# GpSimd as a third elementwise engine, another charge for its overlap with VectorE, and k/q turned by two f32 matmuls

## The chip, the cores and the metric

The kernel runs on one core of a Trainium2 chip. A core has TensorE (matmuls, whose weights are loaded by instructions of their own), VectorE, ScalarE, GpSimd, and SyncE, which here issues every DMA. The metric is the time of one execution on the device in microseconds. The profile calls the engines PE (and PEld for the loads of weights), DVE, ACT, POOL and SP.

## The reference

Attention with a soft cap feeds a two-layer block with a leaky activation. There are 4 batches, 12 heads, 448 positions, a head size of 64, a model width of 768 and an inner width of 2048; all inputs are f32.

```python
scores = scale * np.matmul(q, k.transpose(0, 1, 3, 2))
scores = cap * np.tanh(scores / cap)
scores = scores - np.max(scores, axis=-1, keepdims=True)
attn = np.exp(scores)
attn = attn / (np.sum(attn, axis=-1, keepdims=True) + 1e-09)
x = matmul(attn, v), heads laid side by side: 1792 x 768
h = x @ w_in
g = np.maximum(h, 0.0) + alpha * np.minimum(h, 0.0)
out = g @ w_out
```

## The kernel before

**Precision.** Most products are done in f16 with each operand split in two: hi is the f16 value of the scaled operand, lo the f16 value of what hi misses. A product is then three matmuls, hi with hi, hi with lo and lo with hi. So q, k, v, the probabilities, w_in, w_out, the attention output and the activation g all pass through a split. There are two ways to split. The direct one scales and rounds to hi (`scaled`), then makes lo with one VectorE operation that scales, subtracts and rounds (`split_lo`, L389). The indirect one scales in place in f32 (`scaled`), copies to hi (`copy`), and subtracts (`minus`, L386), which GpSimd may do as well as VectorE. `QA`, `VA`, `AI` and `AO` say which share of the tensors of q/k, of v, of w_in and of w_out goes the direct way; `share(i, x)` spreads it evenly. In the kernel before, q/k, w_in, w_out and the probabilities are all direct, v half.

**Batch 0** is computed in f32 (`attention32`), because its units come before much else can run. A unit is a pair of heads in one of two parts of the sequence (192 and 256 rows). `turn` (L449 to L455) brings k and q from rows to columns: for each chunk of 112 rows one transpose on TensorE for the first head (L454) and one f32 matmul with the identity for the second (L455), which puts it on the other half of the output partitions. The scores are f32 matmuls (L666). The probabilities are turned by f32 matmuls with a diagonal matrix that also scales them (`turn_32`, L561), and multiplied with v in f32 (`PV_32`, L611). `PD_A` and `PD_B` say from which pair on, in each part, a unit takes the f16 way instead: with 5 in the second part it is the last of its six pairs.

**Batches 1 to 3** (`attention`, 18 units) split q and k into the tile nat, turn it by one DMA transpose into qkTs, form the scores from it in f16 (L724), take tanh, maximum, exp and sum (`steps`, L508, L513, L515, L520, L525), split each block of 128 rows of probabilities into pw (`turn_split`), and turn pw by DMA transposes into ptall, from which `PV_split` (L597) makes the output with the split v.

**The block after it.** `mm1` (L741) makes h for 128 inner columns at a time, 18 matmuls each, then scales, applies the activation (L751), and splits into gall. `mm2` (L782) makes the output rows from gall and w_out. The weights come in with `w_in_chunks` and `w_out_all`: the words are turned into f32 (L837, L841, L847), scaled by norms (L861), and split in `split_w`.

**The order of the work** is written out when the program is built. Every piece of work is handed to `Plan.op` with a priority, a table of engines that may do it and its cost there in ns, and the regions that it reads and writes. `Plan.order` plays this through as an event simulation: a free engine takes the ready piece of lowest priority number, with a penalty (`PEN`, `PEN2`) added where VectorE is one of several choices; `emit` then issues the instructions in that order on the engines chosen. All DMAs are on SyncE's queue in the planned order. While TensorE has nothing ready, up to a planned time `FILL_END`, the planner gives it filler matmuls (L991) that nobody reads. A VectorE piece has `port=True` unless it reads PSUM or reduces; in the kernel before the plan lets such a piece and a GpSimd piece follow one another but never overlap. On the chip only semaphores for data hold the engines back.

Of the kernel before, what the change touches and what calls it, by code (L numbers as in the profile page):

```python
# [26 lines left out]
PD_B = 5  # L27
MQ = 3
AQ = 3
PEN = 593.1  # L30
PEN2 = 357.34
B0_P = -21.6
LD_P = -4.13
LO_P = -146.94
MM_P = 766.13
X_P = 30.7
ST_P = -12.3
ST1_P = 9.3
PV_P = 53.98
QK_P = -5.54  # L40
V_P = 27.5
WI_P = 31.8
WI_S = 4.16
A_S = 12.4
MM1_P = 6.26
WO_P = 75.25
WO_S = 5.62
WT_P = -127.9
WT_S = -15.47
B1_P = 46.83  # L50
B_S = 32.07
EVAC_P = 201.2
# [7 lines left out]
AI = 1  # L60
AO = 1
PW = 3
QA = 1.0
VA = 0.5
FILL_END = 365429.37
# [10 lines left out]
class Plan:  # L76
# [42 lines left out]
    def order(self):  # L119
# [8 lines left out]
        port = {"dve": 0.0, "pool": 0.0}  # L128
# [23 lines left out]
        def put(o):  # L152
            for e in o.times:
                heapq.heappush(ready[e], (o.prio + ((PEN if "act" in o.times else PEN2) if len(o.times) > 1 and e == "dve" else 0.0), o.idx, o))

# [8 lines left out]
        while todo:  # L164
            while events and events[0][0] <= now:
                _, _, kind, x = heapq.heappop(events)
                if kind == 0:
                    for y in x.next:
                        y.deps -= 1
                        if not y.deps:  # L170
                            put(y)
                elif kind == 1:
                    banks.append(x.slot)
                    used[x.kind] -= 1
            for e in free:
# [3 lines left out]
                while ready[e]:  # L179
# [14 lines left out]
                    if e == "sp":  # L194
                        issue, wait, t = t
                        dma = max(now + wait, dma) + t
                        end = dma + 1000.0 - LAT
                        lanes = lanes[1:] + [dma + 1000.0]
                        free[e] = max(now + issue, lanes[0])
                    else:  # L200
                        free[e] = end = run_pe(t, o.rows) if e == "pe" else now + t
                        if e == "pool":
                            free[e] = end = port[e] = max(now, port["dve"]) + t
                        elif e == "dve" and o.port:
                            port[e] = end
# [3 lines left out]
                    seq += 1  # L209
                    heapq.heappush(events, (end + LAT, seq, 0, o))  # L210
                    for h in o.handles:
                        h.ops.remove(o)
                        if not h.ops:
                            seq += 1
                            heapq.heappush(events, (end + LAT, seq, 1, h))
# [22 lines left out]
def kernel(  # L238
# [39 lines left out]
    alph = ct([P, NF], F32, "alph")  # L278
    n_wi = ct([P, NF], F32, "n_wi")
# [4 lines left out]
    sg = ct([P, NF], F32, "sg")  # L284
    cs_g = ct([P, NF], F32, "cs_g")
    ca_g = ct([P, NF], F32, "ca_g")
# [104 lines left out]
    def either(n, psum=False):  # L391

        return {"act": 220 + 0.85 * n, "dve": 170 + (1.05 if psum else 0.5) * n}
# [143 lines left out]
    def turn_split(u, pr, n, c, t, tr, f, fr):  # L537
# [5 lines left out]
        op(pr, {"act": 640, "dve": 470}, lambda e: scaled(e, hi, t, f), r=[*tr, fr], w=[wt[0]])  # L543
        op(pr, {"dve": 680}, lambda e: split_lo(lo, t, f, hi), r=[*tr, fr, wt[0]], w=[wt[1]])
# [6 lines left out]
    def turn_32(u, pr, n, c, t, tr, f, fr):  # L551
# [4 lines left out]
        op(pr, either(P), lambda e: scaled(e, d, ident, f), r=[identr, fr], w=[dr])  # L556
# [12 lines left out]
    def split(prio, raw, rr_, sv, st, hi, hr, lo, lr, direct):  # L569

        if direct:
            op(prio, two, lambda e: scaled(e, hi, raw, sv), r=[rr_, st], w=[hr])
            op(prio, {"dve": 740}, lambda e: split_lo(lo, raw, sv, hi), r=[rr_, st, hr], w=[lr])
            return
        op(prio, two, lambda e: scaled(e, raw, raw, sv), r=[st], w=[rr_])
        op(prio, two, lambda e: copy(e, hi, raw), r=[rr_], w=[hr])
        op(prio, {"pool": 1370, "dve": 650}, lambda e: minus(e, lo, raw, hi), r=[rr_, hr], w=[lr])
# [7 lines left out]

    two = {"act": 710, "dve": 485}

    def PV_split(u, prio, n, vs, vt):
# [11 lines left out]
        op(prio, {"pe": 12 * (n / 2.4 + 3)}, PV, r=vt + [("pt", u.po[x], u.po[x] + 4 * n) for x in range(2)], w=[h])  # L600
# [17 lines left out]
    def xout(u, prio, h, w, o, sc, sr=()):  # L618
# [7 lines left out]
        op(prio, either(w, True), part(lambda e, pv: scaled(e, hi, pv, sc)), r=[h, *sr], w=[xr(u.b, u.pair, 0, o, w)], port=False)  # L626
        op(prio, {"dve": 247 + 0.82 * w}, part(lambda e, pv: split_lo(lo, pv, sc, hi)),
# [4 lines left out]
    def attention32(part, pair):  # L632
# [6 lines left out]
        if part == 0:  # L639
            h = plan.handle("a")  # L640
            rk, rkr = raw32[4, pair]
            op(prio, {"pe": 1720}, lambda e, h=h: turn(h, rk, 0, NCH), r=[rkr, identr], w=[h], rows=0.7)
# [9 lines left out]
        op(prio, {"pe": 430 * nch}, lambda e, h=h: turn(h, rq, c0, nch), r=[rqr, identr], w=[h, qr], rows=0.7)  # L652
# [26 lines left out]
    def attention(b, pair):  # L679
# [47 lines left out]
        steps(u, prio, S, S_, lambda c: 430 if c == 3 else 380, [qt], [sc, amt], True)  # L727
# [5 lines left out]
    def mm1(b, j, o, n, prio):  # L733
# [16 lines left out]
        op(pr, either(n, True), lambda e: scaled(e, t, ps_p[h.slot][:, :n], cs_g[:, j:j + 1]), r=[h] + sgt, w=[tt], port=False)  # L750
# [3 lines left out]
        for src, to, m in pieces:  # L754
# [3 lines left out]
            op(pr + 10, either(m), lambda e, hi=hi, a=a: copy(e, hi, t[:, a]), r=[tt], w=[gh])  # L758
            op(pr + 10, {"pool": 420 + 1.6 * m, "dve": 160 + 0.97 * m}, lambda e, hi=hi, lo=lo, a=a: minus(e, lo, t[:, a], hi),
# [15 lines left out]
    def mm2(b, t, hf, prio):  # L775
# [19 lines left out]
        op(EVAC_P + prio * 1e-4, either(NH, True), lambda e: scaled(e, osb[:, cols], ps_p[h.slot][:, :NH], osc),  # L795
# [80 lines left out]
    def split_w(prio, dst, dr, flat, fr, s, sr, direct):  # L876
        space, a, z = dr
        high, low = (space, a, (a + z) // 2), (space, (a + z) // 2, z)
        if direct:
            op(prio, {"act": 930, "dve": 545}, lambda e: scaled(e, dst[:, :DM], flat, s), r=[fr, sr], w=[high])  # L880
            op(prio, {"dve": 960}, lambda e: split_lo(dst[:, DM:], flat, s, dst[:, :DM]), r=[fr, sr, high], w=[low])
# [49 lines left out]


# [106 lines left out]
```

## Time and profile before

| | |
|---|---|
| median of 3 runs | 751.47 us (751.47 to 752.59) |
| span of the profiled execution | 749.1 us |
| TensorE busy | 718.3 us, 96% |
| VectorE busy | 514.4 us, 69% |
| ScalarE busy | 450.0 us, 60% |
| GpSimd busy | 156.6 us, 21% |

The profiled execution's own time is given by its span, from the first to the last instruction; the runs are timed around the whole launch. Busy is the time in which an engine has an instruction in work. A matmul in the pipeline counts until its modelled end, so TensorE can show as busy with short gaps inside. Fillers count as busy.

### The profile page before, as it was taken

To read this page: it belongs to the slowest core of one execution; us is meant where nothing else is said; L and a number is where in the kernel's file an instruction comes from. 1 tells how busy PE (TensorE), PEld (TensorE's weight loads), DVE (VectorE), ACT (ScalarE), POOL (GpSimd) and SP (SyncE) were. 2 spreads that over 40 slices of the span, in tenths; PEclk is the share of its full clock that TensorE was granted. 3 is DMA by queue.
4 is the path that set the end of the run, shared out by engine and by line. 5 is a ranking of instruction groups with operands and counts; after the bars stand their busy time and mean duration, and the time that the engine had idled before them with its cause. 6 is when DMAs were issued, how large, how long until landed. Compare 5 with 4: busy or idle time off the path is not lost.

```text
span 749.1 us, 13417 instructions
## 1 busy us (share of the span) xinstructions
PE 718.3 (96%) x5043; PEld 446.5 (60%) x5043; DVE 514.4 (69%) x1021; ACT 450.0 (60%) x893; POOL 156.6 (21%) x286
## 2 busy tenths in 40 slices
PE   9999999967987999999999999999999999999997
PEld 5776576656865875566545556555455555555664
DVE  2889889898897888867787787777877642452000
ACT  3768778874796786577775666688576632231010
POOL 1012112141442241102434211213343100000000
PEclk9999999998999999999999999999999999999999
DMA  9956525576988647998648699998736960000001
GB/s 213 279 177 210 163 92 179 95 186 165 188 154 181 99 100 152 192 182 159 114 87 160 123 192 213 179 176 137 145 72 118 157 120 1 21 1 1 22 22 42
DMA packets 227936, 98.66 MB, mean 132 GB/s; under 512 B 191456, under 2 KB 224160, under 8 KB 227872
## 3 DMA queue, kind: packets, MB, share of 16 engines
q1 hardware_dynamic: 227872, 97.82, 62.1%
q8 instruction: 39, 0.64, 0.4%
q14 instruction: 25, 0.20, 0.1%
HBM read 45.82 MB, written 5.51 MB: 69 GB/s over the span
## 4 chain that ended last, share of the span: by engine, by line
PE 83%; DMA 8%; DVE 5%; ACT 2%; issue 1%; POOL 0%; SPq 0%; ACTq 0%; POOLq 0%
PE p L782 27%; PE p L741 25%; PE s L724 6%; PE p L597 5%; DMA ptall<-pw 4%; PE p L561 4%; PE s L666 4%; PE p L991 4%; DMA qkTs<-nat 3%; PE p L611 2%; PE p L455 2%; PE p L454 1%; PE p L861 1%; PE p L365 1%; DVE wi L389 1%
## 5 line engine op out<-in xcount | busy, mean ns | idle before, releaser
L741 PE MATMUL p<-xring,wi 128*128 128x448 f16 (+2 forms) x1440 | 229.1, 319 | 6.5 <-DVE gr L751 5.8
L782 PE MATMUL p<-wp,gall 128*128 128x384 f16 x1344 | 225.3, 326 | 0.0
L741 PEld LDWEIGHTS <-wi 128*128 128x128 f16 x1440 | 137.6, 99 | 93.7 <-issue 11.7
L782 PEld LDWEIGHTS <-gall 128*128 128x128 f16 x1344 | 129.9, 98 | 90.6 <-issue 5.7
L389 DVE SCALAR_TENSOR_TENSOR pw<-tall,rr,pw 128x448 f16<-128x448 f32 x126 | 88.0, 716 | 17.7 <-ACT pw L381 16.8
L520 ACT ACTIVATE tall<-tall,mxs,small 128x448 f32<-128x448 f32 x126 | 94.2, 751 | 7.2 <-POOL mxs L515 7.1
L386 POOL TENSOR_TENSOR gall<-gr,gall 128x192 f16<-128x192 f32 (+4 forms) x76 | 63.5, 845 | 124.7 <-ACT gall L375 83.8
L515 POOL TENSOR_SCALAR mxs<-mxs,small 128x2 f32<-128x2 f32 (+1 forms) x90 | 44.5, 495 | 212.8 <-DVE mxs L513 161.6
L381 ACT ACTIVATE pw<-tall,rr 128x448 f16<-128x448 f32 x100 | 64.5, 661 | 38.1 <-DMA ptall<-pw 23.6
L751 DVE SCALAR_TENSOR_TENSOR gr<-p,ca_g,gr 128x448 f32<-128x448 f32 (+2 forms) x80 | 46.9, 587 | 49.6 <-ACT gr L381 48.9
L508 ACT ACTIVATE tall<-s,ams 128x896 f32<-128x896 f32 (+1 forms) x72 | 64.6, 906 | 17.9 <-PE s L724 14.6
L513 DVE TENSOR_REDUCE mxs<-tall 128x2 f32<-128x896 f32 x72 | 68.5, 961 | 5.1 <-ACT tall L508 4.5
L381 ACT ACTIVATE gr<-p,cs_g 128x448 f32<-128x448 f32 (+2 forms) x59 | 32.7, 554 | 58.0 <-PE p L741 53.9
L724 PE MATMUL s<-qkTs 128*128 128x448 f16 (+1 forms) x288 | 59.8, 357 | 7.2 <-ACT gall L375 3.9
L525 POOL TENSOR_SCALAR rr<-sums 128x2 f32<-128x2 f32 (+1 forms) x96 | 35.2, 367 | 118.4 <-ACT tall L520 87.6
L375 ACT ACTIVATE gall<-gr 128x384 f16<-128x384 f32 (+4 forms) x84 | 35.3, 437 | 32.7 <-DVE gr L751 32.4
L381 ACT ACTIVATE wp<-p,small 128x384 f32<-128x384 f32 x22 | 12.8, 580 | 62.3 <-PE p L782 62.2
L597 PE MATMUL p<-ptall,vs 112*64 112x448 f16 (+1 forms) x456 | 46.8, 350 | 0.4 <-DMA ptall<-pw 0.4
L724 PEld LDWEIGHTS <-qkTs 128*128 128x128 f16 (+1 forms) x288 | 21.7, 100 | 30.4 <-issue 10.2
L666 PE MATMUL s<-tall,qkTs 128*128 128x448 f32 x84 | 37.3, 570 | 1.2 <-ACT gall L508 1.2
L597 PEld LDWEIGHTS <-vs 112*64 112x64 f16 x456 | 25.9, 110 | 18.8 <-issue 5.5
L991 PE MATMUL p<-ident 128*128 128x128 f16 x513 | 34.0, 226 | 2.8 <-POOL ident masks.py:199 1.7
(139 smaller groups left out, 843.5 us busy)
## 6 DMA issues: line engine op xcount, KB each, us to landing
wp<-in_moe_w_in_dram SPq DMA_DIRECT2D x16, 768.0 KB, 5.2
wp<-in_moe_w_out_dram SPq DMA_DIRECT2D x16, 768.0 KB, 5.0
rvs<-in_v_dram SPq DMA_DIRECT2D x38, 224.0 KB, 3.3
rqk<-in_q_dram SPq DMA_DIRECT2D x18, 224.0 KB, 3.2
rqk<-in_k_dram SPq DMA_DIRECT2D x18, 224.0 KB, 3.5
ptall<-pw SPq DMA_TRANSPOSE x148, 3.3
wp<-in_k_dram SPq DMA_DIRECT2D x6, 224.0 KB, 7.4
wp<-in_q_dram SPq DMA_DIRECT2D x6, 224.0 KB, 6.2
```

Source lines behind the costliest of these rows:

```text
L381: nc.scalar.activation(out=o, in_=i, func=AF.Copy, scale=s)
L386: (nc.gpsimd if e == "pool" else nc.vector).tensor_tensor(out=o, in0=a, in1=b, op=ALU.subtract)
L389: nc.vector.scalar_tensor_tensor(out=o, in0=i, scalar=s, in1=hi, op0=ALU.mult, op1=ALU.subtract)
L508: op(pr, {"act": 245 + 377 * m}, lambda e, s=s, t=t, m=m: nc.scalar.activation(out=t, in_=s[:, :m, :S].rearrange("p c (j k) -> p c j k", j ...
L513: op(pr, {"dve": 136 + 469 * m}, lambda e, mt=mt, t=t: nc.vector.tensor_reduce(out=mt, in_=t, axis=AX.XY, op=ALU.max), r=tr, w=[mr], port= ...
L520: nc.scalar.activation(out=t[:, x], in_=t[:, x], func=AF.Exp, scale=capt, bias=mt[:, x:x + 1], accum_out=u.sums[:, c:c + 1])
L597: nc.tensor.matmul(pv[x * D:(x + 1) * D, :n], vs[:, z, c:c + D], u.pt[x][:CP, y * NCH + kc], start=(i == 0), stop=(i == len(prods) - 1))
L666: steps(u, prio, n, lambda s, c: nc.tensor.matmul(s, qz[:, c * P:(c + 1) * P], kt[:, pair], start=True, stop=True), lambda c: 750, [qr, kt ...
L724: nc.tensor.matmul(s[rows], qT[:, x * S + cols.start:x * S + cols.stop], qkT[:, r0:r0 + NCH, :], start=(z == 0), stop=(z == 1))
L741: nc.tensor.matmul(ps_p[h.slot][:, :n], w[:, z, kk, :], x[:, d, o:o + n], start=(kk == 0 and z == d), stop=(kk == NPAIR - 1 and z == 1))
L782: nc.tensor.matmul(ps_p[h.slot][:, :NH], g[j][:, d, t * P:(t + 1) * P], w[:, z, hf * NH:(hf + 1) * NH], start=(j == 0 and z == d), stop=(j ...
L991: nc.tensor.matmul(ps_p[slot][:, :P], ident.bitcast(F16)[:, :P], ident.bitcast(F16)[:, P:], start=True, stop=True)
```

## The change

1. `turn` uses an f32 matmul with the identity for both heads, each on its half of the output partitions, in place of a transpose and a matmul.
2. `copy` and `scaled` can run on GpSimd, and the costs of copies, scalings and differences (`either`, `diff`) offer GpSimd for the splits of q, k, v, the probabilities, the weights and the diagonals, and for the hi of g. Operands in PSUM stay with ScalarE and VectorE.
3. The plan lets GpSimd and VectorE overlap, and lengthens the GpSimd piece by 0.7 of the overlap.
4. `AI` and `QA` go from 1 to 0, so that w_in, q and k are split the indirect way, and a new `PA` of 0.5 sends half of the blocks of probabilities that way. `PD_B` goes from 5 to 6, so that all of batch 0 is done in f32.
5. The priorities, penalties and costs of the plan have new values, which gives a new order throughout.

```diff
-PD_B = 5
+PD_B = 6
-PEN = 593.1
-PEN2 = 357.34
+PEN = 835.22
+PEN2 = 87.08
+PENP = 114.65
...
-AI = 1
+AI = 0
-QA = 1.0
+QA = 0
 VA = 0.5
+PA = 0.5
+SHARED = 0.7
...
-                    if not fits(o) or e == "dve" and o.port and port["pool"] > now:
+                    if not fits(o):
...
+                    if e == "pool":
+                        pool = now + t + SHARED * min(t, max(0.0, dve_port - now))
+                        free[e] = math.inf
...
+                    if e == "dve" and o.port:
+                        dve_port = end
+                        if pool:
+                            pool += SHARED * min(t, max(0.0, pool - now))
...
     def copy(e, o, i):
-            nc.vector.tensor_copy(o, i)
+            (nc.gpsimd if e == "pool" else nc.vector).tensor_copy(o, i)
...
+        elif e == "pool":
+            nc.gpsimd.tensor_scalar(out=o, in0=i, scalar1=s, scalar2=1.0, op0=ALU.mult, op1=ALU.mult)
...
-        return {"act": 220 + 0.85 * n, "dve": 170 + (1.05 if psum else 0.5) * n}
+        t = {"act": (170 if psum else 200) + 93 * f + 0.833 * n, "dve": 155 + 50 * f + 1.05 * n if psum else 175 + 65 * f + 0.47 * n}
+        if pool:
+            t["pool"] = 240 + 0.87 * n
+        return t
...
+    def diff(n, direct):
+        return {"dve": 220 + 1.03 * n} if direct else {"pool": 176 + 1.92 * n, "dve": 161 + 1.04 * n}
...
-            a, c = slice(i * CP, (i + 1) * CP), c0 + i
-            nc.tensor.transpose(tp[:D, a], r[:, c * D:(c + 1) * D], ident[:CP, :CP])
-            nc.tensor.matmul(tp[D:, a], r[:, (NCH + c) * D:(NCH + c + 1) * D], ident[:CP, :CP], start=True, stop=True)
+            for x in range(2):
+                o = (x * NCH + c0 + i) * D
+                nc.tensor.matmul(tp[x * D:(x + 1) * D, i * CP:(i + 1) * CP], r[:, o:o + D], ident[:CP, :CP], start=True, stop=True)
...
-        op(pr, {"act": 640, "dve": 470}, lambda e: scaled(e, hi, t, f), r=[*tr, fr], w=[wt[0]])
-        op(pr, {"dve": 680}, lambda e: split_lo(lo, t, f, hi), r=[*tr, fr, wt[0]], w=[wt[1]])
+        direct = share(blk_no[0], PA)
+        if direct:
+            op(pr, either(S, f=True, pool=True), lambda e: scaled(e, hi, t, f), r=[*tr, fr], w=[wt[0]])
+            op(pr, diff(S, True), lambda e: split_lo(lo, t, f, hi), r=[*tr, fr, wt[0]], w=[wt[1]])
+        else:
+            op(pr, either(S, f=True, pool=True), lambda e: scaled(e, t, t, f), r=[fr], w=tr)
+            op(pr, either(S, pool=True), lambda e: copy(e, hi, t), r=tr, w=[wt[0]])
+            op(pr, diff(S, False), lambda e: minus(e, lo, t, hi), r=[*tr, wt[0]], w=[wt[1]])
...
-        op(prio, {"dve": 545, "act": 930}, lambda e: scaled(e, flat, flat, s), r=[sr], w=[fr])
-        op(prio, {"act": 837, "dve": 545}, lambda e: copy(e, dst[:, :DM], flat), r=[fr], w=[high])
-        op(prio, {"pool": 1990, "dve": 945}, lambda e: minus(e, dst[:, DM:], flat, dst[:, :DM]), r=[fr, high], w=[low])
+        op(prio, either(DM, f=True, pool=True), lambda e: scaled(e, flat, flat, s), r=[sr], w=[fr])
+        op(prio, either(DM, pool=True), lambda e: copy(e, dst[:, :DM], flat), r=[fr], w=[high])
+        op(prio, diff(DM, False), lambda e: minus(e, dst[:, DM:], flat, dst[:, :DM]), r=[fr, high], w=[low])
```

## Rows read from the trace of the kernel before

**Rows 1.** The page: span, and busy us, share and instructions of each engine.
```profile
span 749.1 us, 13417 instructions
PE 718.3 (96%) x5043; PEld 446.5 (60%) x5043; DVE 514.4 (69%) x1021; ACT 450.0 (60%) x893; POOL 156.6 (21%) x286
```

**Rows 2.** Windows: stretch, length, busy of PE, PEld, DVE, ACT, POOL; clock; DMA.
```profile
0.00:150.00 150.00, 143.46 (x1058) 101.00 (x1060) 119.70 (x232) 108.02 (x223) 26.35 (x67) 0.99 0.64 176
150.00:285.00 135.00, 115.40 (x1125) 90.60 (x1122) 117.35 (x221) 97.39 (x195) 45.92 (x62) 0.95 0.73 151
285.00:350.00 65.00, 65.00 (x494) 39.22 (x493) 49.66 (x112) 43.83 (x87) 10.62 (x26) 1.00 0.92 180
350.00:640.00 290.00, 289.70 (x1767) 156.41 (x1764) 206.09 (x408) 181.04 (x356) 73.69 (x132) 1.00 0.72 132
```

**Rows 3.** The chain that ended last, its two last long pieces: start, us, what.
```profile
638.12 44.26 PE p L741 x234
682.38 62.41 PE p L782 x384
```

**Rows 4.** Windows of the fillers alone: stretch, length, busy of PE and PEld.
```profile
0.00:150.00 150.00, 10.38 (x124) 9.05 (x124) 0.99 0.64 176
150.00:285.00 135.00, 16.50 (x268) 15.51 (x268) 0.95 0.73 151
285.00:350.00 65.00, 7.09 (x121) 6.84 (x121) 1.00 0.92 180
```

**Rows 5.** Groups of PE by shape: busy us, mean ns, idle before them.
```profile
L454 PE MATMUL p<-ident,wp 112*64 112x112 f32 x54 | 15.3, 283 | 0.0
...
L597 PE MATMUL p<-ptall,vs 112*64 112x256 f16 x24 | 1.5, 278 | 0.0
```

**Rows 6.** Timeline of PE, two of the first turns: start, us, instruction.
```profile
6.35 0.29 PE L454 MATMUL p<-ident,wp 112*64 112x112 f32 x1
...
10.78 0.29 PE L454 MATMUL p<-ident,wp 112*64 112x112 f32 x1
```

**Rows 7.** The chain in batch 0: f32 products of two kinds.
```profile
45.62 0.91 PE p L561 x8
...
96.23 1.45 PE p L611 x16
...
131.32 1.88 PE p L611 x16
```

**Rows 8.** Groups of DVE by shape: the direct lo of three kinds.
```profile
L389 DVE SCALAR_TENSOR_TENSOR pw<-tall,rr,pw 128x448 f16<-128x448 f32 x126 | 88.0, 716 | 17.7 <-ACT pw L381 16.8
...
L389 DVE SCALAR_TENSOR_TENSOR nat<-rqk,ams,nat 112x512 f16<-112x512 f32 x36 | 28.2, 798 | 1.4 <-ACT nat L381 1.1 <-PE p L611 0.3
...
L389 DVE SCALAR_TENSOR_TENSOR wi<-wi,s_wi,wi 128x768 f16<-128x768 f32 x14 | 13.8, 1008 | 0.0
```

**Rows 9.** Groups of POOL by shape: a difference of 512 columns.
```profile
L386 POOL TENSOR_TENSOR vs<-rvs,vs 112x512 f16<-112x512 f32 x8 | 10.6, 1331 | 9.2 <-ACT vs L375 8.6 <-POOL rr L525 0.4
```

**Rows 10.** Lines 389 and 515: count, least, median and longest ns.
```profile
L389 DVE SCALAR_TENSOR_TENSOR pw<-tall,rr,pw x126: 654/678/1460, 172.6 to 610.1; 128x448 f16<-128x448 f32 x126
...
L389 DVE SCALAR_TENSOR_TENSOR nat<-rqk,ams,nat x36: 730/744/1654, 112.2 to 580.5; 112x512 f16<-112x512 f32 x36
...
L515 POOL TENSOR_SCALAR mxs<-mxs,small x90: 267/268/1807, 13.8 to 601.1; 128x2 f32<-128x2 f32 x68, 128x1 f32<-128x1 f32 x22
```

**Rows 11.** Groups of ACT by shape: a scaled copy of 512 columns.
```profile
L381 ACT ACTIVATE nat<-rqk,ams 112x512 f16<-112x512 f32 x22 | 15.2, 712 | 5.4 <-DVE ams L342 3.6 <-PE p L611 1.7
```

**Rows 12.** Groups of DVE from 150 to 285 us alone.
```profile
L389 DVE SCALAR_TENSOR_TENSOR pw<-tall,rr,pw 128x448 f16<-128x448 f32 x27 | 18.4, 689 | 4.0 <-ACT pw L381 3.7
...
L389 DVE SCALAR_TENSOR_TENSOR nat<-rqk,ams,nat 112x512 f16<-112x512 f32 x8 | 6.8, 894 | 0.0
```

**Rows 13.** The tile nat: who waited for what follows it (us, times).
```profile
  PEld L724: 7.1, 4
  PE s L724: 2.2, 3
```

More of the change, by code (lines that the diff above doesn't have):

```diff
@@ L26 @@
 PD_A = 6
-PD_B = 5
+PD_B = 6
 MQ = 3
 AQ = 3
-PEN = 593.1
-PEN2 = 357.34
[L32 to L52, printed above, removed]
+PEN = 835.22
+PEN2 = 87.08
+PENP = 114.65
+B0_P = -23.09
+LD_P = -29.96
+LO_P = -302.09
+MM_P = 941.15
+X_P = 7.27
+ST_P = -3.74
+ST1_P = 24.86
+PV_P = -12.41
+QK_P = -25.73
+V_P = 17.66
+WI_P = 72.0
+WI_S = 3.74
+A_S = 8.89
+MM1_P = 88.84
+WO_P = 108.62
+WO_S = 7.54
+WT_P = -487.61
+WT_S = -76.6
+B1_P = 21.4
+B_S = 30.32
+EVAC_P = 3.08
 LAT = 200.0
@@ L126, in order @@
         warm, win, busy = False, 0, 0.0
-        port = {"dve": 0.0, "pool": 0.0}
+        pool, dve_port = None, 0.0
         def gate(t):
@@ L153, in put, with landed @@
             for e in o.times:
-                heapq.heappush(ready[e], (o.prio + ((PEN if "act" in o.times else PEN2) if len(o.times) > 1 and e == "dve" else 0.0), o.idx, o))
+                pen = 0.0 if len(o.times) == 1 else PENP if e == "pool" and "act" in o.times else PEN if e == "dve" and "act" in o.times else PEN2 if e == "dve" else 0.0
+                heapq.heappush(ready[e], (o.prio + pen, o.idx, o))
+        def landed(o, end):
+            nonlocal seq
+            seq += 1
+            heapq.heappush(events, (end + LAT, seq, 0, o))
+            for h in o.handles:
+                h.ops.remove(o)
+                if not h.ops:
+                    seq += 1
+                    heapq.heappush(events, (end + LAT, seq, 1, h))
         def fits(o):
@@ L174, in order @@
                     used[x.kind] -= 1
+                elif kind == 3:
+                    if pool > now:
+                        seq += 1
+                        heapq.heappush(events, (pool, seq, 3, x))
+                    else:
+                        pool, free["pool"] = None, now
+                        landed(x, now)
             for e in free:
@@ L201, in order @@
                         free[e] = end = run_pe(t, o.rows) if e == "pe" else now + t
[L202 to L205, printed above, removed]
                     started.append((now, o.fn, e))
@@ L208, in order @@
                     todo -= 1
[L209 to L215, printed above, removed]
+                    if e == "pool":
+                        pool = now + t + SHARED * min(t, max(0.0, dve_port - now))
+                        free[e] = math.inf
+                        seq += 1
+                        heapq.heappush(events, (pool, seq, 3, o))
+                        break
+                    if e == "dve" and o.port:
+                        dve_port = end
+                        if pool:
+                            pool += SHARED * min(t, max(0.0, pool - now))
+                    landed(o, end)
                     if free[e] > now:
@@ L555, in turn_32 @@
         d, dr = diags[:, i], ("dg", i, i + 1)
[L556 removed]
+        op(pr, either(P, f=True, pool=True), lambda e: scaled(e, d, ident, f), r=[identr, fr], w=[dr])
         h = plan.handle("a")
@@ L598, in PV @@
                                      start=(i == 0), stop=(i == len(prods) - 1))
-        op(prio, {"pe": 12 * (n / 2.4 + 3)}, PV, r=vt + [("pt", u.po[x], u.po[x] + 4 * n) for x in range(2)], w=[h])
+        op(prio, {"pe": 12 * (n / 2.4 + 12)}, PV, r=vt + [("pt", u.po[x], u.po[x] + 4 * n) for x in range(2)], w=[h])
         return h
@@ L624, in part @@
             return lambda e: fn(e, ps_p[h.slot][:, :w])
-        op(prio, either(w, True), part(lambda e, pv: scaled(e, hi, pv, sc)), r=[h, *sr], w=[xr(u.b, u.pair, 0, o, w)], port=False)
-        op(prio, {"dve": 247 + 0.82 * w}, part(lambda e, pv: split_lo(lo, pv, sc, hi)),
+        op(prio, either(w, True, f=bool(sr)), part(lambda e, pv: scaled(e, hi, pv, sc)), r=[h, *sr], w=[xr(u.b, u.pair, 0, o, w)], port=False)
+        op(prio, {"dve": 160 + 50 * bool(sr) + 1.04 * w}, part(lambda e, pv: split_lo(lo, pv, sc, hi)),
            r=[h, *sr, xr(u.b, u.pair, 0, o, w)], w=[xr(u.b, u.pair, 1, o, w)], port=False)
```

39 lines of the change are left out of this document (20 added, 19 removed).

## The prediction, made before the change was run

> **What bounds the kernel now.** I read the page's busy shares first: TensorE 96% of a 749.1 us span, VectorE 69%, ScalarE 60%, GpSimd 21% [rows 1]. A mean of this kind hides stages, so the second view was the table of stretches [rows 2]. From 285 us on TensorE has no gap worth the name (65.00 of 65, 289.70 of 290), and the last 106 us are two unbroken pieces of the chain of waits, 44.26 us of first products and 62.41 us of second products [rows 3]. Nothing an elementwise engine does there can make the end earlier. Before 285 us it is otherwise: TensorE lacks 6.5 us in the first 150 and 19.6 us in the next 135, and part of what counts as busy is filler, matmuls that the planner puts in to hold the clock and whose result nobody reads: 10.38 us before 150, 16.50 to 285, 7.09 to 350 [rows 4]. So the kernel has 26 + 34 = 60 us in which TensorE does nothing useful, nearly all before 350 us. In just those stretches VectorE is busiest: 119.70 of 150 (80%) and 117.35 of 135 (87%), against 71% from 350 to 640. ScalarE has 72% in both, GpSimd 18% and 34%.
>
> The time can therefore fall in two ways: useful TensorE work is taken away, or the 60 us are closed up by feeding TensorE sooner before 350 us. Between 285 us and the end a stall that a new wait makes costs its full length.
>
> The sum below is made against the span of the profiled execution, 749.1 us; the runs have 751.47 us, so 2.4 us lie around the span, and I add them at the end. About 0.2% (1.5 us) is what runs of this kernel can tell from no change.
>
> **The turning of k and q.** A chunk (112 rows, two heads) is now one transpose (L454, one instruction) and one f32 matmul (L455, two instructions). There are 54 chunks, as the count of L454 says [rows 5]. In the first run of them eight chunks go from 6.35 to 10.78 us, 0.554 us each [rows 6]; so all take 54 x 0.554 = 29.9 us of TensorE. After the change a chunk is two f32 matmuls, four instructions, on the two halves of the output partitions. The nearest row is the product L611, the same shape of weights (112x64 f32) on the same two halves: 16 instructions in 1.45 us at 192 columns (0.091 each) and in 1.88 us at 256 (0.118) [rows 7]. That these halves run side by side is seen against L561, f32 at full width: 8 instructions of only 128 columns take 0.91 us, 0.114 each. Half the columns, the same interval. The line through the two L611 points (0.42 ns a column) gives 0.057 us at 112 columns, 0.228 a chunk. Lower end of the gain: the halves don't overlap and an instruction costs what L561 costs, 0.114 x 112/128 = 0.100, or 0.40 a chunk. So the change saves between 54 x 0.154 = 8.3 us and 54 x 0.326 = 17.6 us. I take 17.6, since L611 is the same instruction but for its length.
>
> **PD_B 5 to 6.** The last pair of the second part of batch 0 leaves the f16 path and takes the f32 one. Gone: four blocks' scaled copy and lo (VectorE 0.716 each [rows 8]), four transposes by DMA, the split of v, and a product of 24 instructions, 1.5 us [rows 5]. New: four times eight L561 instructions (4 x 0.91 = 3.6 us), a product L611 at 256 columns (1.88 us [rows 7]), four diagonals and four copies out of PSUM. TensorE pays +4.0 us; VectorE gets back about 3.4 us.
>
> Both edits lie before 175 us, and most before 150, where TensorE is busy or filling 143 of 150 us, so the difference of -13.6 us counts in full if VectorE keeps up. It does: by 150 us it loses the lo of about 13 w_in chunks (13 x 1.008 = 13.1 us [rows 8]), about 4 us of lo of q and k and the 3.4 us above, and gets back at most 13 copies. 119.7 less 20.5 plus some 7 is 106 in a stage of 136: 78%, the share it has now. If the cover were gone (all added passes on VectorE) a few us of the 13.6 would be lost.
>
> **AI 1 to 0, QA 1 to 0, PA 0.5, and GpSimd as a choice.** Each split that was "scaled hi, then lo in one VectorE operation" becomes three operations: scale in place, copy to f16, difference. The difference may go to GpSimd, the other two to GpSimd, ScalarE or VectorE. It concerns all 16 w_in chunks, 36 tensors of q and k, and half of 130 blocks of probabilities. VectorE can lose 16 x 1.008 = 16.1, 36 x 0.798 = 28.7 and 65 x 0.716 = 46.5 us, 91 us in all; 117 extra passes come in (16 + 36 + 65). GpSimd pays 1.331 us for a difference of 512 columns [rows 9], by length 2.0 for 768; so at most 16 x 2.0 + 101 x 1.33 = 166 us if it takes them all, on top of 157. It has the room. No row has a wide one-input pass on GpSimd; it lies between the least that GpSimd takes for two columns (0.267 us [rows 10]) and the two-input difference of the same width (1.331). I take 1.0, nearer to the wide row than to the tiny one; at that price it does not pay GpSimd to take all 117, and ScalarE (0.712 at 512 columns [rows 11]) takes most.
>
> What this is worth is read from 150 to 285 us. There VectorE has 27 lo of probabilities (half of them, 13.5 x 0.69 = 9.3 us), eight lo of q and k (6.8 us) [rows 12] and the last three of w_in (3 us): 19 us of 117 can leave. The extra passes (about 22) cost VectorE 0.45 us each where they land on it, 10 us at most. Net it is 9 to 19 us lighter, and at a constant 87% that is 10 to 22 us of stage. But ScalarE gets part of the extra passes and DMA at 73% does not move, so I take 10 us; the ends are 0 and 30 (half of all 60 idle and filler us).
>
> **Overlap charge.** The planner formerly held back VectorE's port operations while GpSimd ran; now it lets them start and lengthens GpSimd alone. The rows bear that out mostly: GpSimd's tiny L515 goes from 0.267 to 1.807 us [rows 10], while VectorE's L389 on pw has 0.654/0.678/1.460 (min, median, max) and on nat 0.730/0.744/1.654 [rows 10]. So VectorE is hit too, but rarely: mean over median is 38 ns x 126 + 54 ns x 36 = 6.7 us in all. I price it at nothing, since the hit operations themselves become fewer.
>
> The Trainium skill, in "SBUF — State Buffer", section "SBUF: two separate sides", says otherwise: the port pair that the two engines share is an exclusive lock, taken for a whole instruction, and whoever comes second stands still, VectorE too when it reads two SBUF inputs. The maxima above agree that it happens; the medians say that it seldom decides. By that rule more wide GpSimd work would cost VectorE, and the time would be that of the second rival below.
>
> **Sum.** 749.1 - 13.6 - 10 = 725.5 us, plus 2.4: 728 us.
>
> **Rivals.**
> Only the matmuls count. GpSimd's wide time goes up two- to threefold, and with it the 6.7 us that VectorE loses to it, to some 13 to 20 us; with the extra passes that eats the 9 to 19 us. For it: in 150 to 285 GpSimd's work already lies beside VectorE at 87%. Against it: the medians. 749.1 - 13.6 + 2.4 = 738 us.
> The halves don't run side by side when two different small matmuls meet: -8.3 + 4.0 - 10, so 737 us. Against it: L611.
> Everything closes up: half of the 60 us go, 30 in place of 10: 708 us. For it: VectorE can shed up to 91 us and it is the engine ahead of TensorE in each gap. Against it: early gaps also wait for DMA, and a schedule with two full engines seldom closes.
> Slower: the chain to the scores of batches 1 to 3. One tensor of q or k took ScalarE 0.712 and VectorE 0.798; now it takes 0.712 for the scaling, no more than that again for the copy, and 1.331 on GpSimd, 1.25 us more, and the second tensor's difference stands behind the first's on GpSimd, 0.53 more: 1.8 us later for each of 18 units, and behind it the transpose by DMA. TensorE runs in a fixed order, so a late qkTs stops it. Today TensorE's loads and matmuls already wait for it in seven places, 9.3 us [rows 13], so the slack is not large. With all 18 late: 738 + 32 = 770; it decides against the change from 8 of 18 on (13.6 / 1.8). With 12 late: 738 + 21.6 = 760 us. Against it: the loads are asked for a unit ahead, and VectorE, which did this work, gets freer.
>
> **Numbers.** 728 us: 0.43 (its own range 718 to 737). Only the matmuls, 738: 0.17. No overlap of halves, 737: 0.08. All closes up, 708: 0.17. Slower, 760: 0.12. That the new order comes out about where it was, gain and stalls in balance: 0.03. Faster by over 0.2%: 0.84; within 0.2%: 0.03; slower: 0.13. The range goes to 711 below (half of the 708 case is left out) and to 748 above (the slower case is left out).
>
> **What would show it.** A chunk of the turning at 0.23 us and some 216 instructions on its line; useful TensorE work less by 13 to 14 us; fillers and gaps before 350 us at about 50 instead of 60; VectorE under 500 us in all, GpSimd at 300 us or more; TensorE without gaps from about 270 us on. Wrong: chunks at 0.4 us; VectorE's two-input operations with means well over their medians; TensorE waiting for qkTs or ptall after 350 us.

## Result and the profile after

The changed kernel takes 728.25 us (median of 4 runs, 724.98 to 728.97) against 751.47 us: a ratio of 0.968, 95% interval 0.965 to 0.971. The forecast was 728 us. The sum came out; the profile shows that one of its two terms came about in another way than the forecast said.

The page of the changed kernel, as in [rows 1]:
```profile
span 726.5 us, 14070 instructions
PE 709.4 (98%) x5276; PEld 452.1 (62%) x5276; DVE 522.6 (72%) x1021; ACT 422.8 (58%) x835; POOL 345.1 (48%) x457
```
GpSimd has more than doubled, ScalarE has lost 27 us, and VectorE is not lighter but 8 us heavier, in a span that is 23 us shorter.

The stretches of [rows 2] (stretch, length, busy us and instructions of PE, PEld, DVE, ACT, POOL; granted clock, DMA share, GB/s):
```profile
0.00:150.00 150.00, 144.44 (x1308) 113.33 (x1310) 128.65 (x247) 113.98 (x239) 92.50 (x127) 0.98 0.75 203
150.00:285.00 135.00, 129.93 (x1322) 100.77 (x1317) 127.78 (x226) 94.70 (x184) 90.03 (x96) 0.99 0.70 142
285.00:350.00 65.00, 65.00 (x422) 35.67 (x421) 52.18 (x113) 41.93 (x81) 34.84 (x54) 1.00 0.82 153
350.00:640.00 290.00, 288.03 (x1746) 154.86 (x1745) 202.47 (x412) 160.08 (x313) 127.73 (x182) 1.00 0.69 126
```
TensorE's gaps before 285 us fall from 26.1 us to 5.6 + 5.1 = 10.6. The fillers alone, as in [rows 4], rise from 34.0 to 45.7 us:
```profile
0.00:150.00 150.00, 13.36 (x175) 11.97 (x175) 0.98 0.75 203
150.00:285.00 135.00, 29.77 (x456) 26.94 (x456) 0.99 0.70 142
285.00:350.00 65.00, 2.58 (x37) 2.11 (x37) 1.00 0.82 153
```
So gaps and fillers together fall only from 60.1 to 56.3 us: most of what had been gaps is now filler. The end is as in [rows 3], two unbroken pieces, with 7 us more of the first products left for it:
```profile
608.51 51.07 PE p L776 x270
659.58 62.41 PE p L817 x384
```

The turning, as in [rows 6] (start, us, instruction); eight chunks, four instructions each, between two products of scores:
```profile
10.60 1.75 PE L485 MATMUL p<-ident,wp 112*64 112x112 f32 x32
12.28 1.02 PE L701 MATMUL s<-tall,qkTs 128*128 128x448 f32 x2
```
From 10.60 to 12.28 us is 0.21 us a chunk, where it was 0.554 [rows 6] and 0.228 was forecast. The groups of TensorE show the rest of the edits to batch 0 (line, operation, shapes, count | busy us, mean ns):
```profile
L597 PE MATMUL p<-diags,gall 128*112 128x128 f32 x280 | 37.1, 284 | 0.1
...
L485 PE MATMUL p<-ident,wp 112*64 112x112 f32 x216 | 13.0, 267 | 0.0
...
L597 PE MATMUL p<-diags,ptall 128*112 128x128 f32 x56 | 6.9, 274 | 0.0
...
L646 PE MATMUL p<-ptall,xring 112*64 112x256 f32 x16 | 1.9, 386 | 0.0
```
The 32 new instructions that turn probabilities and the one new product stand here; the f16 product of [rows 5] is gone.

VectorE, the groups that answer to [rows 8] and some that stand beside them:
```profile
L412 DVE SCALAR_TENSOR_TENSOR pw<-tall,rr,pw 128x448 f16<-128x448 f32 x63 | 46.1, 732 | 11.7 <-ACT pw L402 10.5 <-POOL pw L404 1.0
...
L876 DVE SCALAR_TENSOR_TENSOR wp<-wp,wp 128x768 int32<-128x768 int32 x18 | 22.1, 1230 | 0.0
...
L412 DVE SCALAR_TENSOR_TENSOR wp<-wp,s_wo,wp 128x768 f16<-128x768 f32 x16 | 19.2, 1234 | 0.0
...
L741 DVE COPY nat<-nat 112x1024 f16<-112x1024 f16 x18 | 11.5, 638 | 0.1
...
L412 DVE SCALAR_TENSOR_TENSOR vs<-rvs,vam,vs 112x512 f16<-112x512 f32 x9 | 10.0, 1111 | 0.0
```
and their least, median and longest time, as in [rows 10]:
```profile
L412 DVE SCALAR_TENSOR_TENSOR pw<-tall,rr,pw x63: 662/676/1449, 136.9 to 571.4; 128x448 f16<-128x448 f32 x63
...
L412 DVE SCALAR_TENSOR_TENSOR wp<-wp,s_wo,wp x16: 1002/1012/1912, 241.7 to 268.0; 128x768 f16<-128x768 f32 x16
...
L412 DVE SCALAR_TENSOR_TENSOR vs<-rvs,vam,vs x9: 736/745/2439, 168.7 to 547.9; 112x512 f16<-112x512 f32 x9
...
L876 DVE SCALAR_TENSOR_TENSOR wp<-wp,wp x18: 920/945/2416, 88.9 to 229.1; 128x768 int32<-128x768 int32 x18
```
The medians are those of before; the means have left them. For these four groups mean less median, times the count, is 3.5 + 3.6 + 3.3 + 5.1 = 15.5 us in which VectorE stands behind GpSimd. Taken the same way over all of VectorE's groups, it is 9.3 us before and 50.0 us here; busy time less this is about 505 us before and 473 us here. That GpSimd is the cause can be counted: of the 332 VectorE instructions with no GpSimd instruction beside them not one took over 0.1 us more than the median of its group, of the 689 with one 98 did.

One such stand is seen to reach TensorE (start, us, instruction, idle time before it):
```profile
91.78 1.64 POOL L409 TENSOR_TENSOR wi<-wi,wi 128x768 f16<-128x768 f32 x1
91.81 2.42 DVE L876 SCALAR_TENSOR_TENSOR wp<-wp,wp 128x768 int32<-128x768 int32 x1
...
95.06 0.56 DVE L381 TENSOR_SCALAR mxt<-ident,mxt 4x4 f32<-4x4 f32 x1
...
95.68 0.58 PE L386 MATMUL p<-mxt,ones 4*128 4x4 f32 x2 [2.97 <-DVE mxt L381]
```
L876 takes 2.42 us where its median is 0.945, L381 comes behind it on VectorE, and TensorE stands idle for 2.97 us, its longest wait for another engine. From 95.00 to 101.83 us its granted clock is 0.50, the lower of its two levels, 1.2 GHz:
```profile
95.00:101.83 6.83, 6.15 (x21) 5.05 (x22) 6.03 (x13) 2.26 (x5) 3.99 (x3) 0.50 1.06 230
```
Whether the clock would have stayed up without the 1.5 us that L876 lost is not shown.

GpSimd's own passes of 512 columns, as in [rows 9], now with the one-input kind that no row of before had:
```profile
L409 POOL TENSOR_TENSOR nat<-rqk,nat 112x512 f16<-112x512 f32 x15 | 21.7, 1448 | 14.1 <-ACT nat L396 11.1 <-DVE nat L398 2.6
...
L404 POOL TENSOR_SCALAR rqk<-rqk,ams 112x512 f32<-112x512 f32 x15 | 11.6, 775 | 6.7 <-issue 4.5 <-DVE ams L363 0.8 <-DVE vam L466 0.8
```

And what TensorE's score products of batches 1 to 3 wait for (us, times), which answers to [rows 13]:
```profile
its engine sat idle before it (us, times) until:
  issue: 10.3, 25
  ACT tall L538: 1.2, 1
```
No DMA is among them any more.

### The profile page after: what moved, and what is told of

It reads as the page before. It is cut to its first block, busy times and chain, and to the rows that moved or that the text cites. A ratio compares the mean times of both kernels' runs of the same rounds, so it can differ in the third digit from the quotient of the medians.

```text
span 726.5 us, 14070 instructions
## 1 busy us (share of the span) xinstructions
PE 709.4 (98%) x5276; PEld 452.1 (62%) x5276; DVE 522.6 (72%) x1021; ACT 422.8 (58%) x835; POOL 345.1 (48%) x457
## 5 line engine op out<-in xcount | busy, mean ns | idle before, releaser
L543 DVE TENSOR_REDUCE mxs<-tall 128x2 f32<-128x896 f32 (+1 forms) x72 | 68.7, 956 | 1.7 <-ACT tall L538 1.2
L409 POOL TENSOR_TENSOR pw<-tall,pw 128x448 f16<-128x448 f32 x37 | 43.9, 1188 | 29.5 <-ACT pw L396 17.2
L545 POOL TENSOR_SCALAR mxs<-mxs,small 128x2 f32<-128x2 f32 (+1 forms) x66 | 39.3, 595 | 38.8 <-DVE mxs L543 25.3
L409 POOL TENSOR_TENSOR gall<-gr,gall 128x384 f16<-128x384 f32 (+4 forms) x38 | 33.8, 892 | 43.9 <-DVE gall L398 37.8
L412 DVE SCALAR_TENSOR_TENSOR pw<-tall,rr,pw 128x448 f16<-128x448 f32 x63 | 46.1, 732 | 11.7 <-ACT pw L402 10.5
L1024 PE MATMUL p<-ident 128*128 128x128 f16 x668 | 45.7, 225 | 4.7 <-DVE gr L786 1.9
L632 PE MATMUL p<-ptall,vs 112*64 112x448 f16 x432 | 45.7, 355 | 0.7 <-DMA ptall<-pw 0.7
L1024 PEld LDWEIGHTS <-ident 128*128 128x128 f16 x668 | 41.0, 101 | 7.1 <-issue 4.5
L409 DVE TENSOR_TENSOR gall<-gr,gall 128x64 f16<-128x64 f32 (+4 forms) x74 | 36.6, 496 | 2.9 <-POOL gall L398 0.4
L396 ACT ACTIVATE gall<-gr 128x384 f16<-128x384 f32 (+4 forms) x53 | 23.4, 441 | 24.3 <-DVE gr L786 23.9
L597 PE MATMUL p<-diags,gall 128*112 128x128 f32 x280 | 37.1, 284 | 0.1
```

Of the source, the lines that this page charges most:

```text
L409: (nc.gpsimd if e == "pool" else nc.vector).tensor_tensor(out=o, in0=a, in1=b, op=ALU.subtract)
L412: nc.vector.scalar_tensor_tensor(out=o, in0=i, scalar=s, in1=hi, op0=ALU.mult, op1=ALU.subtract)
L543: op(pr, {"dve": 136 + 469 * m}, lambda e, mt=mt, t=t: nc.vector.tensor_reduce(out=mt, in_=t, axis=AX.XY, op=ALU.max), r=tr, w=[mr], port= ...
L632: nc.tensor.matmul(pv[x * D:(x + 1) * D, :n], vs[:, z, c:c + D], u.pt[x][:CP, y * NCH + kc], start=(i == 0), stop=(i == len(prods) - 1))
L1024: nc.tensor.matmul(ps_p[slot][:, :P], ident.bitcast(F16)[:, :P], ident.bitcast(F16)[:, P:], start=True, stop=True)
```

## Experiments

Each run was timed beside the kernel before on its chip, which lay between 750.6 and 751.5 us. Times are medians.

**1. The turning taken back, the order kept.** In the changed kernel:
```diff
-            for x in range(2):
-                o = (x * NCH + c0 + i) * D
-                nc.tensor.matmul(tp[x * D:(x + 1) * D, i * CP:(i + 1) * CP], r[:, o:o + D], ident[:CP, :CP], start=True, stop=True)
+            a, c = slice(i * CP, (i + 1) * CP), c0 + i
+            nc.tensor.transpose(tp[:D, a], r[:, c * D:(c + 1) * D], ident[:CP, :CP])
+            nc.tensor.matmul(tp[D:, a], r[:, (NCH + c) * D:(NCH + c + 1) * D], ident[:CP, :CP], start=True, stop=True)
```


> The changed kernel with one edit taken back: each chunk of k and q is again one transpose and one f32 matmul. The plan is left as it is, so order, engines and all other instructions stay. Theory (the turning is paid in full on TensorE's path): 54 chunks at 0.55 us in place of 0.22, so +17 to +18 us, 745 to 746 us. Rival (TensorE's early gaps and fillers take the saving up): the planned fillers and gaps before 285 us shrink by as much as the chunks grow and the time stays within 5 us of 728.


Measured: 740.85 us, ratio 0.988 (0.984 to 0.991), span 740.9. So the turning is worth 12.6 us by the medians, 14.4 by the spans, not 17 to 18. Part of the difference is the clock. The stretch in which the changed kernel gets a granted clock of 0.83, first the changed kernel, then this one:
```profile
85.00:105.00 20.00, 17.03 (x132) 13.86 (x131) 17.22 (x27) 13.47 (x30) 14.43 (x12) 0.83 0.75 211
```
```profile
85.00:105.00 20.00, 20.00 (x152) 14.98 (x150) 18.14 (x28) 16.95 (x35) 13.46 (x16) 1.00 0.57 172
```
With the short turning TensorE has 3 us of gaps there and runs part of the stretch at the lower level, 1.2 GHz (20 us at 0.83 are 3.4 us of work lost); with the long one it has none and keeps 2.4 GHz. Over the whole span the gaps are alike, 726.5 - 709.4 = 17.1 us in the changed kernel and 740.9 - 723.6 = 17.3 us here. It is the clock that takes part of the saving: its mean in the two profiled executions is 0.993 and 1.000, and 0.007 of 726.5 us is 5.1 us of TensorE's work.

**2. The new turning alone, the order kept.** The same edit the other way round in the kernel before, costs in the plan untouched.

> The kernel before with one edit alone: two f32 matmuls a chunk, nothing else, the plan's costs and so its order unchanged. Theory: TensorE is released 17.6 us sooner in the first 115 us and passes that on where the other engines are not pacing it; VectorE at 80% of that stage leaves room, so 734 to 740 us. Rival (the other engines pace the first stage in the fixed order): under 6 us gained, 746 us or more, and new gaps of TensorE in the first 115 us.


Measured: 742.05 us, ratio 0.989 (0.986 to 0.993): 8.7 us, between the two. TensorE's longest waits (engine, line, tile waited for: us, times, longest):
```profile
PE s L724 <- DMA qkTs<-nat: 7.8, 2, 4.3
PE p L741 <- DVE gr L751: 4.6, 3, 2.5
PE p L861 <- DVE wp L847: 4.4, 2, 3.3
PE p L861 <- DVE wi L847: 3.8, 2, 2.7
```
In the kernel before, two of these waits were:
```profile
PE p L861 <- DVE wp L847: 4.6, 2, 3.5
...
PE s L724 <- DMA qkTs<-nat: 2.2, 3, 1.1
```
About half of the 17.6 us comes back as gaps of TensorE, which grow from 749.1 - 718.3 = 30.8 us to 742.0 - 702.7 = 39.3 us: it now comes early to products whose inputs VectorE has not made (L847, 4.6 us before and 4.4 + 3.8 now) or whose transpose has not landed (2.2 us before, 7.8 now).

**3. The same with the plan told of it.** As 2, and the plan's cost of a chunk 230 ns:
```diff
-            op(prio, {"pe": 1720}, lambda e, h=h: turn(h, rk, 0, NCH), r=[rkr, identr], w=[h], rows=0.7)
+            op(prio, {"pe": 230 * NCH}, lambda e, h=h: turn(h, rk, 0, NCH), r=[rkr, identr], w=[h], rows=0.7)
-        op(prio, {"pe": 430 * nch}, lambda e, h=h: turn(h, rq, c0, nch), r=[rqr, identr], w=[h, qr], rows=0.7)
+        op(prio, {"pe": 230 * nch}, lambda e, h=h: turn(h, rq, c0, nch), r=[rqr, identr], w=[h, qr], rows=0.7)
```


> The kernel before with the new turning, its cost in the plan now 230 ns a chunk, so the order is made anew; nothing else changed. With the order left alone this edit gave 8.7 of 17.6 us. Theory (the rest was lost since the order did not know of it): 734 to 738 us. Rival (VectorE and ScalarE pace batch 0 once TensorE is faster): 741 to 744 us again.


Measured: 751.65 us, ratio 1.001 (0.999 to 1.003). Both theories are wrong: with a cost nearer to the measured one the order came out 9.6 us worse and the gain vanished. Between 150 and 285 us TensorE now lacks 34.5 us (19.6 before), at a granted clock of 0.84.

**4. No one-input passes on GpSimd, all else as changed.**
```diff
-        if pool:
+        if pool and False:
             t["pool"] = 240 + 0.87 * n
```


> The changed kernel without GpSimd as a choice for copies and scalings; differences may still go to it, the three-step splits stay, the plan is made anew. Theory (GpSimd's one-input passes are what lets VectorE and ScalarE carry 117 extra passes): about 100 us of GpSimd's work goes back to the two, and the time is 738 to 750 us. Rival (GpSimd's work only blocks VectorE as much as it relieves it): 728 us within 4.


Measured: 757.64 us, ratio 1.009 (1.006 to 1.013), worse than the kernel before, more than the theory had.

**5. As 4, and all splits direct.**
```diff
-AI = 0
-QA = 0
-PA = 0.5
+AI = 1
+QA = 1.0
+PA = 1.0
```


> The changed kernel with all splits of w_in, q, k and the probabilities direct again and no copies or scalings on GpSimd: what is left of the change is the turning, PD_B, the overlap charge and the new constants, with a new plan. Theory (13 us come from TensorE's own edits and about 9 from GpSimd): 737 to 738 us. Rival (the new constants carry the 9 us): 728 us. Second rival (the constants fit only the three-step splits): over 745 us.


Measured: 754.72 us, ratio 1.005 (1.003 to 1.007). The second rival's number, and 12.7 us above experiment 2, which has the turning in the old order. Its fillers:
```profile
0.00:150.00 150.00, 12.92 (x162) 11.15 (x162) 0.99 0.75 201
150.00:285.00 135.00, 45.92 (x735) 42.62 (x735) 1.00 0.68 140
285.00:350.00 65.00, 10.32 (x165) 9.55 (x165) 1.00 0.86 163
```
69 us in place of 46: the work that TensorE is to do between 150 and 350 us comes later.

**6. The changed kernel with the old priorities and penalties** (PEN to EVAC_P, 23 numbers).

> The changed kernel with the 23 priorities and penalties of the kernel before (PEN to EVAC_P; PENP stays), all else as changed. Theory (GpSimd and the turning carry the gain, the constants fit the order to them): 728 to 738 us. Rival (the constants carry it, GpSimd alone nothing): 740 us or more.


Measured: 769.8 us, ratio 1.026 (1.024 to 1.027).

**7. All splits direct, GpSimd still a choice** (AI, QA and PA at 1, as in 5, without the edit of 4).

> The changed kernel with AI, QA and PA at 1: all splits of w_in, q, k and probabilities direct, GpSimd still a choice for copies and scalings. Theory (moving the lo off VectorE is worth some 10 us beside the choice for hi): between the changed kernel and the one without wide GpSimd work, 735 to 745 us. Rival (the choice for hi is all that counts): 728 us within 4; third possibility (only the lo counts): 752 us or more.


Measured: 753.87 us, ratio 1.004 (1.002 to 1.006), the third possibility by its number. But by then five orders made anew had all lain at 750 us or more, whatever the edit; so none of 3 to 7 can be read as the price of its edit before the price of a new order is known.

**8. The old overlap rule in the changed kernel.**
```diff
-                    if not fits(o):
+                    if not fits(o) or e == "dve" and o.port and pool:
...
-                        pool = now + t + SHARED * min(t, max(0.0, dve_port - now))
+                        pool = max(now, dve_port) + t
...
-                        if pool:
-                            pool += SHARED * min(t, max(0.0, pool - now))
```


> The changed kernel with the overlap rule of the kernel before: in the plan a VectorE operation on the shared ports does not start while GpSimd runs, and GpSimd starts after VectorE's; GpSimd is then not lengthened. Everything else as changed, the order made anew. In the trace VectorE's two-input operations run up to 2.4 us instead of 0.95 beside GpSimd. If that loss matters more than the freedom to overlap: below 726 us, and VectorE's means near their medians. If the freedom is what the gain comes from: 735 us or more.


Measured: 792.75 us, ratio 1.057 (1.055 to 1.059). VectorE is at 500.6 us, the least of all, but fillers take 125.6 us in place of 45.7:
```profile
L1022 PE MATMUL p<-ident 128*128 128x128 f16 x2047 | 125.6, 221 | 1.7 <-POOL ident masks.py:199 1.7
```
VectorE still collides: mean less median, times the count, is 31.1 us over its groups. That TensorE is kept waiting where the plan does not let VectorE run would fit the fillers, but is not shown. How much of the 64 us is the rule and how much the unfitted order, this run doesn't tell.

**9. What a new order costs by itself.**
```diff
-LAT = 200.0
+LAT = 205.0
```


> The changed kernel with one number of the plan changed that stands for no work (LAT, the assumed signal time between engines, 205 ns in place of 200): a new order, the same operations. It measures what a re-made order costs by itself, since each kernel so far whose order was made anew lay at 750 us or more. If orders are robust: 728 us within 4. If the constants are fitted to one order and any re-made one loses it: 740 us or more, and the four re-made orders say nothing on their edits.


Measured: 734.77 us, ratio 0.978 (0.975 to 0.981): 6.5 us for an edit that stands for no work. It lies between the two expectations. Differences of 6 us between kernels with different orders are therefore no evidence on an edit. 26 us and more (4, 5, 6, 7) are more than this and speak for constants that fit the operations and engines they were found for. It is one re-made order; how far others scatter was not measured.

**10. Less of GpSimd's work in the changed order.** `part8` cuts a GpSimd operand to 8 columns a group; it is used in the splits of the probabilities and of v and in the scaling of q and k.
```diff
+    def part8(e, *t):
+        return [x[..., :8] for x in t] if e == "pool" else t
...
-            op(pr, diff(S, False), lambda e: minus(e, lo, t, hi), r=[*tr, wt[0]], w=[wt[1]])
+            op(pr, diff(S, False), lambda e: minus8(e, lo, t, hi), r=[*tr, wt[0]], w=[wt[1]])
...
-    for t in pws:
-        nc.gpsimd.memset(t[:, :, CP:], 0.0)
+    for t in (*pws, vs16):
+        nc.vector.memset(t, 0.0)
```


> The changed kernel in its own order, with GpSimd's wide passes on the probabilities, its scaling of q and k and its split of v cut to 8 of their 64 or 112 columns a group (the rest of those outputs is left out; pw and the f16 v are cleared at the start): some 85 us less work on GpSimd, all waits and queues as they are. In the trace VectorE's two-input operations stand up to 1.5 us behind GpSimd. Theory (that loss and GpSimd's own lateness cost the changed kernel time before 350 us): 3 to 10 us less, 718 to 725 us, VectorE's means for pw and wp near their medians. Rival (TensorE covers it): 728 us within 2.


Measured: 722.67 us, ratio 0.962 (0.960 to 0.965), 5.6 us less, as the theory had it. The page, and VectorE's groups:
```profile
span 720.4 us, 14074 instructions
PE 706.5 (98%) x5276; PEld 449.7 (62%) x5276; DVE 505.9 (70%) x1025; ACT 421.7 (59%) x835; POOL 279.9 (39%) x454
```
```profile
L424 DVE SCALAR_TENSOR_TENSOR pw<-tall,rr,pw 128x448 f16<-128x448 f32 x63 | 43.9, 696 | 9.3 <-ACT pw L402 5.0 <-DMA rqk<-in_q_dram 3.8 <-POOL pw L404 0.2
...
L424 DVE SCALAR_TENSOR_TENSOR wp<-wp,s_wo,wp 128x768 f16<-128x768 f32 x16 | 17.7, 1138 | 0.0
...
L753 DVE COPY nat<-nat 112x1024 f16<-112x1024 f16 x18 | 8.3, 462 | 0.0
```
GpSimd does 65 us less, and VectorE, whose own instructions are the same but for four clearings, is busy 16.7 us less. That is the loss shown directly; mean less median, times the count, falls from 50.0 to 32.2 us over all groups. The means of pw and wp come nearer to their medians (676 and 1009 ns) without reaching them; GpSimd's other wide passes are left as they were. Of the time's 5.6 us only a part is this loss: the mean granted clock is 0.998 here and 0.993 in the changed kernel, which over some 725 us is 3.6 us of TensorE work (over the four runs of each it is 0.995 to 0.998 here and 0.992 to 0.996 there). Whether the clock stayed up because VectorE was sooner, the run doesn't tell.

**11. A fitted order without one-input passes on GpSimd.** As 4, with the priorities, penalties and shares searched anew by shortening the plan (AI 0.5, AO 0.5, QA 0.25, PA 1; MM_P 796.97, WT_P -304.61, MM1_P 136.94 and so on).

> The turning, PD_B 6 and the new cost formulas, without any copy or scaling on GpSimd; the priorities, penalties and shares (AI 0.5, AO 0.5, QA 0.25, PA 1) were searched anew for this case by shortening the plan. With the changed kernel's constants this case took 754.7 us. Theory (GpSimd's one-input passes carry about 10 us and no order replaces them): 736 to 745 us. Rival (a fitted order carries the gain, GpSimd as third engine is not needed): 722 to 732 us.


Measured: 733.52 us, ratio 0.977 (0.974 to 0.979). The case without one-input passes on GpSimd, which took 755 to 758 us with the changed kernel's constants (4 and 5, with other shares), takes 734 with its own. It misses both expectations, by 1.5 us the rival's. Its engines:
```profile
PE 709.9 (97%) x5276; PEld 451.5 (62%) x5276; DVE 523.9 (72%) x1041; ACT 457.1 (63%) x910; POOL 199.3 (27%) x290
```
The two fitted orders thus lie 5.3 us apart, less than the 6.5 us that one re-made order cost in experiment 9: what GpSimd's copies and scalings are worth can't be told from it.

**12. VectorE charged as well, constants searched anew.**
```diff
                     if e == "dve" and o.port:
-                        dve_port = end
                         if pool:
-                            pool += SHARED * min(t, max(0.0, pool - now))
+                            x = min(t, max(0.0, pool - now))
+                            free[e] = end = end + 0.35 * x
+                            pool += SHARED * x
+                        dve_port = end
```


> The changed kernel with VectorE charged too: in the plan a VectorE operation that starts beside GpSimd is lengthened by 0.35 of the overlap, about what the trace of the changed kernel shows for its two-input operations; constants searched anew in the same way (VA came out 0). If the missing charge is why the changed kernel still has 56 us of fillers and gaps: 708 to 720 us. If not: 728 us within 5. If the order is only fitted to the plan and not to the chip: over 735 us.


Measured: 734.59 us (729.14 to 737.02 in five runs), ratio 0.979 (0.976 to 0.981). The added charge and a new search, which also took `VA` to 0, did not beat the changed kernel; the time falls between the expectations.

## Why the prediction was right, and where it was not

**The turning.** Right in size: 54 chunks at 0.21 us in place of 0.554 are 18.6 us, 17.6 were forecast, and the row it was read from (L611, the same shape on the same two halves) was the right one. The rival without overlap of the halves is out.

**PD_B.** By the groups of TensorE, L561 had 33.0 and 7.5 us of busy time and has 37.1 and 6.9, and one product of 1.9 us has taken the place of one of 1.5: some +4 us, as forecast. The groups of before are:
```profile
L561 PE MATMUL p<-diags,gall 128*112 128x128 f32 x248 | 33.0, 282 | 1.7 <-ACT qkTs L375 1.3 <-DVE xring L389 0.4
...
L561 PE MATMUL p<-diags,ptall 128*112 128x128 f32 x56 | 7.5, 277 | 0.0
```
It was not run alone.

**"Counts in full".** This was too much. Back in the old order the turning gives 8.7 us, taken out of the new one it costs 12.6 to 14.4. The cover that the forecast named (VectorE at 80%) was not the whole of it: single products wait for single VectorE operations and for transposes (experiment 2), and the granted clock was lower in the stretch with the gap than without it (experiment 1).

**"Net it is 9 to 19 us lighter", with the overlap "at nothing": the step that failed.** VectorE's load was to fall below 500 us; it rose from 514.4 to 522.6, and before 285 us from 237 to 256. The relief itself came: without what its instructions stand beside GpSimd, VectorE goes from about 505 to 473 us over the span, though it has 1021 instructions before and after, since the passes that came have shorter medians than the lo that went. ScalarE got lighter too, from 893 instructions to 835. What failed is the price of the overlap. The forecast saw 6.7 us of it in two groups and took nothing; over all groups it is 9.3 us before and 50.0 after, so 41 us were lost where 32 were gained. VectorE gets back 16.7 us when 65 us of GpSimd's work are cut away (experiment 10).

The rule that the forecast set aside is borne out. In the changed kernel 15 of VectorE's two-input operations of 768 columns (L412, L876, L882; medians 0.945 to 1.012 us) took more than 1.06 us. All 15 began while a GpSimd instruction was running, and all end 0.80 to 0.82 us after that instruction's end, whether it took 0.52 or 2.08 us. So VectorE waits for the whole of it, and what was said of the kernel before, that only semaphores for data hold the engines back, leaves this out. The Trainium skill, "SBUF — State Buffer", section "SBUF: two separate sides", has the ports that the two engines share as a lock that one of them holds for a whole instruction while the other stands still. The trace agrees with it.

Why the rows of before gave so low a price is shown in part. Their plan kept the two engines apart, and GpSimd had 156.6 us of work. Experiment 5 lets them overlap beside 156.5 us and loses 14.5 us; experiment 8 keeps them apart beside 355.2 us and loses 31.1; the changed kernel lets them overlap beside 345.1 us and loses 50.0. In these orders the loss went with the amount of GpSimd's work more than with the plan's rule.

**The 10 us all the same.** The span fell by 22.6 us. Turning and PD_B explain 14 to 15 at most. Gaps and fillers before 350 us gave 3.8, not 10. The granted clock gave about as much: before 285 us it was 0.99 and 0.95 [rows 2] and is 0.98 and 0.99, which is 150 x 0.01 + 135 x 0.05 = 8.3 us of work lost before and 4.4 after. What brought the two about, GpSimd's help or the new order, is not shown. So the right sum rests on a term whose parts were other than said, and partly on luck of the order: a plan changed in nothing but one assumed delay takes 734.8 us.

**What carried it.** The turning, by experiments 1 and 2 in fixed orders, is the largest part. That GpSimd is needed as a third engine was argued and is not shown: a fitted order without its copies and scalings has 733.5 us. What the runs speak for, as far as the one re-made order of experiment 9 can tell, is that constants and operations belong together: with the operations or engines changed and the constants kept (4, 5, 7), or the constants changed and the rest kept (6), the whole gain is given back.

**The rivals.** The slower one, late qkTs, did not come: TensorE waits for no such transpose any more, though the differences on GpSimd do take longer (1.448 us). "Only the matmuls", 738 us, had the mechanism right (the loss to GpSimd eats the relief), the loss too small (13 to 20 us for 50) and its time 10 us too high. It stands first in the forecast's list; where the forecast says that by the rule of the Trainium skill the time would be that of "the second rival", this one is meant by its mechanism. "Everything closes up" is out.

**Open.** PD_B alone; how short a searched order of the kernel before would be without any of the edits; how experiment 10's gain divides between VectorE's loss and the clock; what GpSimd as a third engine is worth in an order fitted as well without it.

## What to carry to other kernels

Where the order is written out by a planner with fitted constants, an edit and a new order are two changes: run the edit in the old order, run the new order with an edit that stands for nothing, and only then read a difference. A collision's price read from a trace with little of it can come out far too low: 9.3 us of VectorE beside 157 us of GpSimd's work before, 50.0 beside 345 after. Whether an engine is relieved has to be counted with what it waits inside its instructions: VectorE's own passes fell by some 32 us, and its busy time rose by 8.

## What the runs showed of the hardware

Two f32 matmuls of 112x64 weights and 112 columns on the two halves of the output take 0.21 us together, against 0.554 for a transpose and one such matmul. GpSimd scales 512 f32 columns in 0.775 us on average where ScalarE takes 0.712 [rows 11], nearer to it than the 1.0 that was assumed. Which VectorE instructions stand behind GpSimd can be told from the changed kernel's trace: of those with a GpSimd instruction beside them, 98 of 358 SCALAR_TENSOR_TENSOR, TENSOR_TENSOR, TENSOR_SCALAR, COPY and CAST instructions that read SBUF alone took over 0.1 us more than the median of their group; of 137 reductions, 71 reciprocals and 120 others that read PSUM none did. And a faster TensorE can be granted a lower clock: in the profiled executions the same order has 1.00 throughout with the slow turning and 0.83 from 85 to 105 us, behind a gap of 2.97 us, with the fast one.
